# One written order for 1056 kernel steps, replaced by another: a long-convolution mixer and an MLP block on one Trainium2 core

## The chip, the cores and the metric

The kernel runs on one core of a Trainium2 chip. The core has five engines with their own instruction streams: TensorE (PE in the profile; its weight loads are listed as PEld), VectorE (DVE), ScalarE (ACT), GpSimd (POOL) and SyncE (SP). Here SP issues nearly all transfers between the chip's memory and the core's on-chip buffers; POOL issues a few. The metric is device time in microseconds (us) of one execution. Five executions of the kernel before took 307.80, 305.87, 303.96, 307.02 and 307.92 us; the median is 307.02.

## The reference

The sequence has S = 2048 positions, D = 640 channels, and the MLP has F = 1728 hidden channels. All inputs are bf16. Cut to what matters:

```
sa, ca, ga, sb, cb, gb = split(silu(c) @ w_mod, 6)       # six vectors of 640
h  = layernorm(x) * (1 + ca) + sa
# A: a long convolution
q  = h
k_shift = sum over t in 0..3 of k[s - 3 + t] * shift_k[:, 3 - t]
kv = k_shift * v
y  = irfft(rfft(kv, 4096) * rfft(ssm_k, 4096))[:2048] + kv * ssm_D
x  = x + ga * (q * y)
h  = layernorm(x) * (1 + cb) + sb
# B: two residual MLPs
u  = gelu(layernorm(h) @ w1)       # 640 -> 640
u  = four channel groups of u, shifted by +1, -1, +2, -2 positions
h  = h + u @ w2
h  = h + gelu(layernorm(h) @ w3) @ w4                    # 640 -> 1728 -> 640
x  = x + gb * B(h)
```

## The kernel before

**An order written out by hand.** The kernel's code first adds 1056 *steps* to a planner. A step is one or a few instructions on one engine, with the regions of the buffers that it reads and writes. The string ORDER (lines 26 to 67) then lists all steps as number and engine: S for SP, G for POOL, D for DVE, A for ACT, P for PE; behind a PE step stands the quarter of PSUM (0 to 3) that it allocates. The planner only replays that string. The costs in the code, such as `add("PE", 0.17 * kn, ...)`, were used when orders were searched, and issue nothing. So each engine runs its steps strictly in the order of the string: a step that waits for its data holds all later steps of that engine, and for SP that means all later transfers. Some steps name two engines in the code (for instance `("ACT", "DVE")`); the letter in the string chooses.

**Buffers.** Nearly all memory is a few large tiles that are used again and again: Ra (ssm_k first, then x), Rb, T01 (DFT data, at the end w3 and w4), R3 (a spectrum, then modulation weights, then activations), R5 (k and v, then a spectrum, then h), RG (a table for the DFT, later w1, w2 and a scratch row), RH, RK and RQ. A transfer into a tile waits until the last reader of the old content is done.

**The stages, in the order in which they start.**

1. *Tables and the spectrum of ssm_k* (0 to about 28 us). ssm_k is loaded, each of its five blocks of 128 channels is transposed by DVE (L395), and a DFT of length 4096 is done in two matmul stages: stage 1 (L408) and stage 2 (L425), each evacuated from PSUM by ACT or DVE (L208, L210). POOL builds tables and the diagonal matrices for the shift.
2. *k_shift and kv* (about 20 to 60). SP loads k and v with transposing transfers, one for each of five blocks (L234; blocks 0 to 4). PE applies the four taps with diagonal weights (L480), DVE multiplies by v (L485), DVE transposes (L395), and the two DFT stages follow (L408, L446). x is loaded by eight transfers of 320 KB (L540; four for tiles 0 to 7, four for 8 to 15), and statistics of the first layer norm are made by ACT or DVE (L554, L562) and finished on POOL (L572 to L577).
3. *Modulation*. w_mod is loaded in 12 pieces of 400 KB (L503), each multiplied by silu(c) on PE (L509) and evacuated (L516 to L526). Six go early. The last six, into R3, are i6 and i7 (for 1 + cb), i8 and i9 (sb), i10 and i11 (gb).
4. *Inverse stage 1* (69.6 to 94.5). For ten blocks, halves of the spectrum are swapped by two transfers (L629, one from SP, one from POOL), DVE makes two products (L633, 20 in all), PE multiplies by tables (L644, L645), and the result is evacuated into T01.
5. *Inverse stage 2* (L685, 97 to 123). PE turns T01 into y, in groups of two or three of the 16 row tiles: 0 to 2, 3 and 4, 14 and 15, 8 to 10, 5 to 7, 11 to 13.
6. *The chains.* The row tiles form groups of one or two. For each, chain a makes x + q*y (L761, L764) and a sum of squares on ACT (L753); ln_finish (L720 to L743) turns sums into mean and scale on POOL, or partly DVE; chain b applies cb and sb (L775, L779, L780); chain c normalizes again (L748, or L610) and turns the tile. The first groups are turned by PE (L796, with a copy, L802), the later ones by a transposing transfer from SP (L789).
7. *The MLPs.* w1 (L842, and L852 for a remainder of the channels), w2 with shifted columns (L897), its residual on DVE (L904), another layer norm and turn, w3 (L931) with gelu on ACT (L935), w4 (L961, L952), the residual (L984), gb and x (L989, L990), and four output transfers for each tile (L993). The very last tile is done in two halves (L1005 to L1011). w1 is loaded into RG at L661, w2 at L662, with four tails at L664, and w3 and w4 into T01 at L1020 to L1023.

The end of a planner's run is a plain replay:

```
order = pl.run()
with tc.manual_schedule():
    for t in order:
        t.fn(t.on)
```

Of the kernel before, what the change touches and what calls it, by code (L numbers as in the profile page):

```python
# [23 lines left out]
LFFT = 4096  # L24

ORDER = """
0S 2S 19G 18D 21G 20D 27G 29D 23D 4S 50G 28D 24A 36G 37G 22D 30A 68G 69D 25A 26G 88P:0 31A 89A 86P:1 87A 56G 90P:2 91A 72G 84P:3 5S 85A 3S 38G 39G 40A
73D 104P:0 106P:1 107A 70D 6S 49G 71D 105D 98P:2 102P:3 103A 99A 8S 118P:0 74G 94P:1 95A 75D 114P:3 115A 108P:2 109A 9S 119D 112P:0 113A 1S 66D 116P:1
41G 42G 43G 67D 80P:3 81A 117D 51D 52D 110P:2 44A 45D 10S 111D 96P:0 97A 82P:1 122P:3 11S 123D 32G 34G 54A 33S 53A 83A 76P:0 77A 100P:2 101D 92P:1 93A
78P:3 7S 120P:0 46G 136D 79A 55G 121D 175P:2 176A 47S 195P:1 196A 35S 179P:3 180A 185P:2 186D 147P:1 141P:0 193P:3 142D 148A 57G 58G 181P:2 182D 59G  # L30
139P:1 194A 140A 201S 199P:0 48S 200A 143P:3 144D 155P:2 165P:1 166D 156A 161P:0 162A 202S 191P:3 192D 12S 157P:2 158A 167P:1 168D 13S 163P:0 164A
197P:3 198A 145P:2 203S 146D 189P:1 65G 151P:0 152D 169P:3 190A 204S 183P:2 170A 184D 159P:1 160A 177P:0 178D 153P:3 154A 173P:2 174A 149P:1 150D
137P:0 260P:3 254D 171P:2 187P:1 138A 60A 188A 61G 62G 63G 261A 214D 172A 14S 124P:0 266P:1 210D 267A 125D 126P:3 127D 15S 211D 255D 209A 258P:2 259A
16S 270P:1 271A 130P:0 131D 268P:3 64A 262P:2 343G 269A 263A 215A 128P:1 264P:3 129D 256D 276P:2 277A 265A 134P:0 132P:1 17S 135D 282P:2 212A 283A
133D 216G 286P:3 223S 224P:0 220S 213G 278P:1 287D 225A 226S 279A 232S 284P:2 257D 221P:0 229S 285A 272P:3 227P:1 222A 228D 274P:2 235S 275D 273A
290P:0 291A 469D 288P:1 289A 233P:3 234D 292P:2 293A 294P:0 296P:3 230P:1 297A 298P:2 295D 299A 466D 342S 253G 246S 248G 312P:0 308P:3 309A 231D 463D
300P:1 301A 313D 460D 251G 310P:2 311D 367G 243S 306P:0 307A 316P:3 317D 280P:1 281A 252G 314P:2 304P:0 302P:3 305A 249S 240G 315D 236P:1 303A 237D
318P:2 319D 467D 340P:0 345D 241S 341A 338P:1 339A 238S 242G 326P:3 327A 344D 245S 250G 366S 322P:2 334P:0 352D 330P:1 331D 323A 244G 335A 239G 247G
324P:3 325A 346P:2 350S 351G 353D 347A 348P:0 360D 320P:3 349A 321A 328P:1 329A 354P:2 355A 359G 358S 361D 374S 356P:0 368D 369D 332P:3 333A 375G
362P:1 363A 364P:2 376D 365A 336P:3 337A 370P:1 371A 357A 372P:2 377D 378P:3 379A 380P:1 381A 383G 382S 385D 384D 386P:0 390S 391G 392D 393D 398S 373A  # L40
388P:3 387A 217A 399G 401D 394P:1 400D 425S 396P:2 397A 408D 407G 389A 402P:0 406S 409D 404P:2 395A 414S 416D 405A 415G 417D 464D 465D 426P:3 403A
427D 452S 410P:1 411A 412P:2 413A 420P:0 421D 418P:1 419A 422S 423P:3 456S 461D 470D 424D 468D 462D 218A 475P:20 477D 476A 520D 459G 454S 499D 500D
471D 521D 472A 540D 434S 219G 523D 541D 543D 437S 438P:1 439A 512A 435P:3 428S 429P:2 430A 431S 432P:0 501A 522A 433A 436A 525D 502G 504D 457S 478P:12
480A 503G 524G 526D 505D 473D 491P:03 545D 542A 544G 507D 553A 492A 527A 474D 546D 479A 571D 568D 485P:20 528G 529G 493A 530D 531P:1 506A 508G 509D
510P:3 486A 208S 547A 487A 458G 511A 548D 549G 481G 569D 570A 572D 573A 482P:20 484A 550D 551P:3 552A 532D 536P:1 533A 513D 537A 207S 574D 483D 575G
576D 580D 577D 517P:0 518A 581D 582D 583A 538P:3 578D 584G 579A 539A 585G 488P:21 489A 556P:0 557A 534D 535D 558P:3 559A 515P:2 516A 453S 514D 631D
632D 633A 586D 589D 590P:0 587P:3 455S 560P:2 634D 206S 635D 637G 591D 636A 638G 554D 561D 563D 588A 639D 562A 600P:0 601A 598P:3 599A 643D 640D 641D
642A 564G 494S 565D 644D 645D 646A 205S 441A 647D 490A 648G 566P:2 498G 567D 444D 651D 555D 605P:0 606D 607A 602P:3 649D 443D 603D 497S 652S 650S 699D
700D 447D 604A 620P:2 621A 495S 616P:1 617A 618P:0 661P:3 619A 662A 659P:2 660A 622P:1 623A 608D 609G 440D 610D 611P:0 613D 614P:3 615D 701A 663P:2
666P:1 664D 612A 683P:3 665A 667D 668A 681P:0 682A 677P:2 445G 656A 653D 654D 442G 655D 592D 669D 670G 674A 678A 671D 672P:1 673D 679P:0 680A 675P:1  # L50
593D 594D 702D 703D 496S 624P:2 595D 596D 676A 519G 597D 765D 749P:0 704A 705G 706G 766D 767A 768D 684A 707A 449A 625D 711D 747P:1 685P:32 712D 748A
769D 713D 714A 708D 709D 715D 771G 626D 446D 770A 710A 745P:1 716G 686P 717A 718S 772G 450D 719D 687D 720S 729P:3 773D 448G 750A 629S 774D 775D 777A
778D 779D 746A 727P:0 721D 781D 722D 723D 834D 835D 780A 776A 730A 627S 451G 790A 787A 657D 658D 782G 783D 743P:1 785D 791D 728A 731P:3 831D 832D 630S
688D 833A 732D 744A 733A 734P:0 735D 784S 786S 793P:1 794A 795P:3 737D 693D 694D 697S 736A 751P:02 796A 797P:1 800P:3 752P 738G 741D 836A 837G 838G
839D 753D 840D 798D 692S 739A 740S 742S 815P:0 843D 844D 801D 803D 841D 696S 813P:1 811P:3 845D 847G 842A 846A 848G 851D 788D 816A 849D 724A 725D 689S
809P:0 799A 852S 802A 804G 807D 814A 810A 812A 805D 850S 853P:1 759D 854A 808S 855P:2 856A 806S 875P:0 876A 869P:3 857P:1 873P:2 871P:0 726D 792D 874A
690S 789D 628S 754D 691S 891D 892D 894D 870A 860P:2 760D 951D 872A 895D 896A 695S 817P:30 893A 897G 898G 952D 954D 861D 862A 858D 863D 877P:21 953A
818P 903A 758S 904D 819D 899D 900D 698S 820D 859A 864G 865A 955G 905D 866S 906A 879D 822S 878P 867A 868S 933P:3 824S 901D 907G 902A 908G 909D 934A
911D 910S 956D 957D 958D 825D 912S 915P:2 935P:0 936A 913P:3 916A 763S 931P:0 757S 959A 914A 917P:2 929P:3 932A 960G 930A 961G 756S 821S 823S 962D
755S 963S 966P:0 967A 918D 919A 826D 885D 886D 920P:2 921D 830S 888S 829S 923G 762S 764S 922A 964P:1 965A 937P:30 969P:2 761S 880D 924G 968G 970D  # L60
972P:1 1003P:2 939D 925A 881S 1004D 926S 973D 975G 927A 928S 987P:3 988A 983P:2 971A 981P:1 890S 984A 1006G 974A 1005A 883S 889S 882S 827S 982A 985P:3
828S 976G 977D 1007G 938P 945D 979A 1008A 978S 980S 1010P:2 1011A 1012P:1 884S 1009S 946D 949S 1016P:0 1017A 948S 940D 942S 944S 1014P:2 943S 986A
989P:03 887S 1013A 1036P:1 991D 992D 996S 994S 1038P:0 990P 1015A 947S 997D 1034P:2 1039A 941S 1018P:03 1035A 1032P:2 1033A 998D 999S 1001S 993S 1002S
1042D 1043D 1000S 950S 1020D 1021D 1025S 1024S 1022S 1023S 1019P 1026D 1037A 995S 1027D 1031S 1029S 1030S 1028S 1040P:02 1044D 1045D 1047S 1046S 1048S
1049S 1041P 1050D 1051D 1052S 1053A 1054S 1055A
"""


# [69 lines left out]
def kernel(  # L138
# [16 lines left out]
    add = pl.add  # L155
# [5 lines left out]
    T01 = mem.tile([P, 20480], BF, name="T01")  # L161
# [272 lines left out]
    def stage2_half(h):  # L434
        for k0 in range(0, 32, 3):
            kn = min(3, 32 - k0)
            ps = Slot()

            def f(e, ps=ps, k0=k0, kn=kn):
                psv = pst(ps, name="ps_s2")[:, :, 0:480].rearrange("p g (k s) -> p g k s", k=3)  # L440
                for j in range(kn):
                    k = k0 + j
                    for cc in range(2):
                        for g in range(2):
                            p = slice(64 * g, 64 * g + 64)
                            nc.tensor.matmul(psv[:, g, j], lhsT=Gs[p, k, 64 - 64 * cc:192 - 64 * cc], rhs=T1h[h][p, cc * 32 + k],  # L446
                                             start=(cc == 0), stop=(cc == 1), tile_position=(64 * g, 0))
            t0 = add("PE", 0.17 * kn, f, r=[("T01", 10240 * h, 10240 * h + 10240), ("RG", 192 * k0, 192 * (k0 + kn))], alloc=ps, ni=8 * kn)
            w = [("R5", 10240 * h, 10240 * h + 10240, "s2"), ("kT", 4 * h, 5, "s2")] + ([("vT", 0, 5, "s2")] if h else [("kTp", 0, 1, "s2")])
            t1 = evac(XS[:, 160 * h:160 * h + 160, k0:k0 + kn, :],  # L450
                      lambda t, kn=kn: t[:, :, 0:480].rearrange("p g (k s) -> p s k g", k=3)[:, :, 0:kn], 320 * kn, ps, w)
# [268 lines left out]
    def ln_finish(li, t0, n, quick):  # L720
# [4 lines left out]
        def f(e):  # L725
            eng_of[e].tensor_scalar(nm, s1, -1.0 / D, None, ALU.mult)  # L726
            if n == 1:
                eng_of[e].tensor_scalar(rs, nm, nm, EPS, ALU.mult, ALU.subtract)
            else:
                eng_of[e].tensor_tensor(rs, nm, nm, ALU.mult)  # L730
                eng_of[e].tensor_scalar(rs, rs, -1.0, EPS, ALU.mult, ALU.add)
# [7 lines left out]
            nc.gpsimd.tensor_tensor(rs, rs, mhalf[:, 0:n], ALU.pow)  # L739
            if not quick:  # L740
                nc.gpsimd.tensor_tensor(nb, nm, rs, ALU.mult)
        add("POOL", 0.8 if quick else 1.1, f, port=-1, r=[("s2", 100 * li + t0, 100 * li + t0 + n), ("nm" + k, 0, 1)], w=[("ln" + k, 0, 1)])
        return rs, nb, ("ln" + k, 0, 1), nm, ("nm" + k, 0, 1), quick  # L743

    def normed(dst, dk, src, sk, rn, i):
# [343 lines left out]
```

## Time and profile before

| what | value |
|---|---|
| median of five executions | 307.02 us |
| profiled execution: time, span | 307.8 us, 306.0 us |
| mean granted TensorE clock | 0.966 |
| PE busy | 270.7 us, 88% |
| DVE busy | 218.1 us, 71% |
| ACT busy | 210.2 us, 69% |
| POOL busy | 111.6 us, 36% |
| moved by DMA | 35.75 MB |
| chain that ended last | PE 57%, DMA 13%, DVE 10%, ACT 6%, POOL 5%, issue 5%, SP 2% |

The span runs from the first to the last instruction of the profiled execution; its time on the device is 1.8 us longer. Times in rows count from the start of the span. A row of the trace gives start, duration, engine, line of the kernel, operation and tiles (written tile before the arrow, read tile behind it); square brackets hold the idle time of the engine before the row and what ended it. Rows "SPq" are SP's issuing of a transfer, which is not the transfer itself. In busy times by stretches, each engine's microseconds stand beside its number of instructions, then the granted clock, the busy share of the 16 DMA engines and GB/s.

### The profile page before, as it was taken

What the parts mean: (1) busy time and instruction counts of PE and PEld (TensorE: products, weight loads), DVE (VectorE), ACT (ScalarE), POOL (GpSimd) and SP (SyncE); (2) the same over time, 40 slices, a digit from 0 to 9 for tenths busy, and PEclk for the clock granted to TensorE, in tenths of its full rate; (3) what the DMA queues carried; (4) which work ended last, traced back from release to release, by engine and by line L of the source; (5) the groups of instructions that cost most, each with busy time, mean ns of one, the idle gap of its engine ahead of it and who ended that gap; (6) DMA issues with size and microseconds to landing.
All of it is one profiled execution on the core that took longest, in us unless ns stands there. A gap on an engine that the chain in (4) does not pass through costs nothing.

```text
span 306.0 us, 7648 instructions
## 1 busy us (share of the span) xinstructions
PE 270.7 (88%) x3050; PEld 207.1 (68%) x3054; DVE 218.1 (71%) x432; ACT 210.2 (69%) x352; POOL 111.6 (36%) x251
## 2 busy tenths in 40 slices
PE   0889999999889458687999989999999999999993
PEld 0555655778787136566887767688867886887771
DVE  8998999999899878879669986656474064031442
ACT  4789999999999599886768776276561752814110
POOL 4968553462104665441525660230152121400000
PEclk9999999999999855899999999999999999999999
DMA  6998999698899910642800222223014123130111
GB/s 200 261 208 181 224 184 270 185 240 217 201 266 272 249 31 3 218 129 48 287 3 1 20 47 51 54 43 77 2 20 85 26 55 70 26 86 5 32 51 43
DMA packets 58116, 35.75 MB, mean 117 GB/s; under 512 B 39873, under 2 KB 54849, under 8 KB 58081
## 3 DMA queue, kind: packets, MB, share of 16 engines
q1 hardware_dynamic: 56768, 31.55, 43.2%
q0 software_dynamic: 1216, 3.67, 4.4%
q8 instruction: 24, 0.39, 0.6%
q14 instruction: 12, 0.09, 0.1%
q10 hardware_dynamic: 96, 0.04, 0.1%
HBM read 16.31 MB, written 2.62 MB: 62 GB/s over the span
## 4 chain that ended last, share of the span: by engine, by line
PE 57%; DMA 13%; DVE 10%; ACT 6%; POOL 5%; issue 5%; SPq 2%; DVEq 0%; ACTq 0%; POOLq 0%
PE ps_w L931 18%; PE ps_w L961 15%; PE ps_w L897 5%; PE ps_ksh L480 4%; PE ps_w L842 4%; PE ps_s L408 4%; DMA R<-in_w_mod_dram 3%; ACT R L208 2%; DMA RG<-R 2%; POOL lnv L739 2%; DMA RK<-R 2%; ACT RG L753 2%; DMA RH<-RK 2%; DMA Rb<-R 2%; DVE Rb L395 1%
## 5 line engine op out<-in xcount | busy, mean ns | idle before, releaser
L931 PE MATMUL ps_w<-R,T 128*128 128x256 bf16 (+1 forms) x630 | 64.6, 261 | 1.2 <-DMA R<-RH 0.7
L931 PEld LDWEIGHTS <-T 128*128 128x128 bf16 x630 | 55.7, 98 | 8.8 <-issue 2.6
L935 ACT ACTIVATE R<-ps_w 128x1024 bf16<-128x1024 f32 (+2 forms) x36 | 29.0, 829 | 47.2 <-PE ps_w L931 47.0
L961 PE MATMUL ps_w<-T,R 128*128 128x320 bf16 x416 | 59.0, 299 | 0.0
L961 PEld LDWEIGHTS <-R 128*128 128x128 bf16 x416 | 40.3, 98 | 15.6 <-issue 0.5
L208 ACT CAST T<-ps_s 128x1024 bf16<-128x1024 f32 x34 | 32.7, 1026 | 3.3 <-PE ps_s L408 3.2
L753 ACT ACTIVATE RG<-R 128x640 bf16<-128x640 bf16 x32 | 23.6, 736 | 13.6 <-DVE R L780 9.0
L408 PE MATMUL ps_s<-F1bd,Rb 128*128 128x256 bf16 x160 | 22.3, 288 | 9.2 <-DVE Rb L395 9.0
L984 DVE TENSOR_TENSOR T<-ps_w,R 128x640 bf16<-128x640 f32 x15 | 12.3, 821 | 22.1 <-PE ps_w L952 11.5
L208 ACT CAST R<-ps_s 128x640 bf16<-128x640 f32 (+1 forms) x36 | 27.3, 844 | 0.8 <-PE ps_s L425 0.6
L408 PEld LDWEIGHTS <-Rb 128*128 128x128 bf16 x160 | 16.2, 103 | 14.9 <-DVE Rb L395 9.8
L897 PE MATMUL ps_w<-RG,R 128*128 128x320 bf16 x160 | 23.7, 302 | 0.0
L739 POOL TENSOR_TENSOR lnv<-lnv,mhalf 128x2 f32<-128x2 f32 (+1 forms) x29 | 22.6, 781 | 2.3
L842 PE MATMUL ps_w<-R,RG 128*128 128x256 bf16 (+1 forms) x200 | 21.1, 268 | 0.6 <-ACT Rb L208 0.5
L726 POOL TENSOR_SCALAR lnv<-stat 128x2 f32<-128x2 f32 (+1 forms) x14 | 4.8, 343 | 44.3 <-DVE Ra L764 17.2
L904 DVE SCALAR_TENSOR_TENSOR R<-ps_w,R 128x640 bf16<-128x640 f32 x16 | 13.0, 819 | 11.2 <-PE ps_w L897 11.2
L644 PE MATMUL ps_i<-EA,Rb 128*128 128x128 bf16 x160 | 19.2, 219 | 1.0 <-DVE Rb L633 0.8
L645 PE MATMUL ps_i<-EB,Rb 128*128 128x128 bf16 x160 | 19.0, 219 | 1.3 <-DVE Rb L633 1.3
L842 PEld LDWEIGHTS <-RG 128*128 128x128 bf16 x200 | 18.0, 107 | 2.7 <-issue 1.2
L897 PEld LDWEIGHTS <-R 128*128 128x128 bf16 x160 | 15.5, 99 | 6.2 <-issue 0.5
L208 ACT CAST T<-ps_i 128x1024 bf16<-128x1024 f32 x19 | 18.2, 1046 | 0.9 <-PE ps_i L645 0.8
L480 PE MATMUL ps_ksh<-R,RQ 128*128 128x512 bf16 x76 | 18.4, 380 | 0.4 <-POOL RQ L356 0.3
(179 smaller groups left out, 522.8 us busy)
## 6 DMA issues: line engine op xcount, KB each, us to landing
Ra<-in_A_ssm_k_dram SPq DMA_DIRECT2D x5, 512.0 KB, 5.4
Ra<-in_A_q_dram SPq DMA_DIRECT2D x8, 320.0 KB, 7.7
R<-in_w_mod_dram SPq DMA_DIRECT2D x6, 400.0 KB, 7.8
out_dram<-RH SPq DMA_DIRECT2D x60, 40.0 KB, 1.6
T<-in_B_w_dram SPq DMA_DIRECT2D x1, 2160.0 KB, 8.7
T<-in_B_w_dram SPq DMA_DIRECT2D x1, 2080.0 KB, 9.9
RH<-in_w_mod_dram SPq DMA_DIRECT2D x4, 400.0 KB, 4.2
RK<-R SPq DMA_DIRECT2D x5, 256.0 KB, 4.3
```

The costliest lines, as they stand in the source:

```text
L208: nc.scalar.copy(dst, src(ps.tile))
L408: nc.tensor.matmul(psv[:, ml, :], lhsT=xL[:, s0:s0 + P], rhs=F1r, start=True, stop=True)
L480: nc.tensor.matmul(pt[:, i, :], lhsT=diagw[:, b, jj, :], rhs=kT[:, b, c0:c0 + 512], start=(jj == 0), stop=(jj == 3))
L644: nc.tensor.matmul(psv[:, w, :], lhsT=Av[:, r_, :, g_], rhs=EAf, start=True, stop=False)
L645: nc.tensor.matmul(psv[:, w, :], lhsT=Bv[:, r_, :, g_], rhs=EBf, start=False, stop=True)
L739: nc.gpsimd.tensor_tensor(rs, rs, mhalf[:, 0:n], ALU.pow)
L753: add("ACT", 0.74, lambda e: nc.scalar.activation(junk, src, ACT.Square, scale=float(D) ** -0.5, accum_out=stat[:, li, 1, t:t + 1]), r=[sk ...
L842: nc.tensor.matmul(pt[:, fb, 0:cw], lhsT=w1_sb[:, b, 160 * fb:160 * fb + P], rhs=hT[:, b, 0:cw], start=(b == 0), stop=(b == ND - 1))
L897: nc.tensor.matmul(pt[:, hf, 0:320], lhsT=gsf[:, fb, c0:c0 + P], rhs=w2_sb[:, fb, 320 * hf:320 * hf + 320], start=(fb == 0), stop=(fb == 4))
L931: nc.tensor.matmul(pt[:, fl, 0:cw], lhsT=w3_sb[:, b, fb * P:(fb + 1) * P], rhs=xT[:, b, 0:cw], start=(b == 0), stop=(b == ND - 1))
L935: nc.scalar.activation(g3[g % 2][:, f0:f0 + fn, 0:cw], ps.tile[:, 0:fn, 0:cw], ACT.Gelu_apprx_tanh)
L961: nc.tensor.matmul(bank(i, hf), lhsT=gg[:, fb, i * P:(i + 1) * P], rhs=w4_sb[:, fb, 320 * hf:320 * hf + 320], start=(fb == 0 and i == 0), ...
```

## The change

ORDER is written out anew: the same 1056 steps, each listed once, in another sequence. Some steps with two possible engines change letter, most PSUM quarters change, and two numbers of the planner's cost table and one unused default argument change with it.

What moves, by the numbers of the steps:

- *SP, around the loads of k and v.* Steps 201 to 204 are the four x loads of tiles 0 to 7, 12 and 13 are k and v block 2, 14 to 17 blocks 3 and 4. Before: 201, 202, 12, 13, 203, 204, 14. After: 201, 204, 203, 202, 12, 13, 14.
- *SP, around the last modulation weights.* Steps 422, 425, 428, 431, 434, 437 are the loads of i6, i7, i8, i9, i10, i11; 414 is the last swap from SP; 452 is w1; 454 to 457 are the tails of w2 and 453 its main part; 205 to 208 are the x loads of tiles 8 to 15; 494 is w3. Before: 414, 452, 422, 456, 454, 434, 437, 428, 431, 457, 208. After: 414, 431, 422, 434, 456, 437, 428, 206, 207, 452, 205, 455, 457, 208, 453, 497, 454, 494. (425 comes earlier in both.)
- *PE, in the same place.* 475, 478, 491, 485, 482 and 488 are groups of inverse stage 2; 423, 426, 429, 432, 435, 438 the modulation products of i6 to i11. Before, from 475 on: 475, 438, 435, 429, 432, 478, 491, 485. After: 475, 435, 432, 438, 478, 429, 491, 485. On ACT, 501 (the first sum of squares of chain a) moves ahead of two evacuations of these products.
- *PE, later.* A w3 step of MLP group 2 (743; groups count from 0) moves ahead of the second w4 tile of group 1 (686), and a w3 step of group 1 (681) behind 749, one of group 2. Both stand before w1 group 5 (729, 727). Near the end of the w1 work, the last w1 group and w2 groups 6 to 8 move ahead of w3 steps of group 5.
- *Engines.* From ACT to DVE: some normalizations and layer-norm statistics (441, 449, 533 among them). From DVE to ACT: four copies of turned tiles (532, 567, 591, 615) and others. From POOL to DVE: seven first parts of ln_finish (528, 584, 637, 847, 897, 907, 975).
- *Start.* On ACT, two evacuations of other blocks of the first DFT come before those of block 0; on POOL one more step stands ahead of the diagonal weights; DVE has more work ahead of its first products.

The core of the diff:

```
 ORDER = """
...
-139P:1 194A 140A 201S 199P:0 48S 200A 143P:3 144D 155P:2 165P:1 166D 156A 161P:0 162A 202S 191P:3 192D 12S 157P:2 158A 167P:1 168D 13S 163P:0 164A
-197P:3 198A 145P:2 203S 146D 189P:1 65G 151P:0 152D 169P:3 190A 204S 183P:2 170A 184D 159P:1 160A 177P:0 178D 153P:3 154A 173P:2 174A 149P:1 150D
...
-427D 452S 410P:1 411A 412P:2 413A 420P:0 421D 418P:1 419A 422S 423P:3 456S 461D 470D 424D 468D 462D 218A 475P:20 477D 476A 520D 459G 454S 499D 500D
-471D 521D 472A 540D 434S 219G 523D 541D 543D 437S 438P:1 439A 512A 435P:3 428S 429P:2 430A 431S 432P:0 501A 522A 433A 436A 525D 502G 504D 457S 478P:12
-480A 503G 524G 526D 505D 473D 491P:03 545D 542A 544G 507D 553A 492A 527A 474D 546D 479A 571D 568D 485P:20 528G 529G 493A 530D 531P:1 506A 508G 509D
...
-769D 713D 714A 708D 709D 715D 771G 626D 446D 770A 710A 745P:1 716G 686P 717A 718S 772G 450D 719D 687D 720S 729P:3 773D 448G 750A 629S 774D 775D 777A
...
+136D 92P:2 34S 47S 120P:3 121D 93A 179P:1 55G 180A 46S 7S 193P:0 194A 35S 195P:2 196A 181P:1 147P:0 148A 182D 201S 141P:3 142D 139P:2 140A 143P:1
+199P:0 175P:3 200A 48S 176A 144D 204S 185P:2 186D 161P:1 162A 65G 157P:0 158D 171P:3 172A 203S 165P:2 166D 191P:1 192A 167P:0 155P:3 156A 168D 169P:2
+170A 177P:1 178D 189P:0 190A 151P:3 159P:2 160A 202S 152D 145P:1 146D 187P:0 188A 149P:3 150D 197P:2 198A 183P:1 184D 153P:0 154A 163P:3 164A 262P:2
+173P:1 174A 12S 137P:0 138A 13S 214D 263A 126P:3 56G 264P:1 210D 254D 127D 57G 124P:0 125D 211D 58G 59G 60A 61G 62G 63G 265A 260P:2 215A 266P:1 267A
+261A 14S 255D 64A 15S 128P:3 129D 258P:0 259A 270P:1 271A 130P:2 131D 256D 16S 212A 276P:0 277A 268P:1 269A 132P:3 134P:2 17S 133D 135D 257D 282P:0
...
+392D 386P:1 400D 387A 396P:2 397A 394P:0 398S 399G 401D 402P:3 425S 403A 404P:1 405A 408D 395A 426P:2 407G 406S 409D 416D 410P:3 415G 414S 417D 412P:1
+431S 411A 465D 413A 461D 462D 427D 216G 420P:0 421D 418P:3 419A 470D 422S 423P:1 424D 471D 468D 218A 475P:20 476A 477D 520D 499D 434S 456S 500D 521D
+540D 541D 543D 459G 472A 435P:3 436A 523D 473D 474D 432P:1 437S 438P:2 219G 501A 433A 512A 478P:03 439A 522A 502G 503G 428S 429P:1 430A 504D 505D 542A
+491P:21 525D 479A 524G 507D 526D 528D 492A 506A 480A 568D 527A 545D 485P:02 487A 493A 486A 206S 544G 546D 547A 207S 508G 509D 510P:3 529G 511A 530D
+531P:2 532A 482P:10 481G 569D 570A 548D 452S 571D 572D 574D 573A 458G 517P:3 518A 205S 513D 536P:2 533D 484D 549G 483A 550D 534D 575G 580D 581D 576D
+455S 582D 457S 577D 578D 208S 514D 538P:3 584D 537A 535D 634D 635D 631D 539A 583A 488P:01 551P:2 552A 579A 585G 586D 515P:3 589D 632D 449D 489A 558P:2
+516A 637D 559A 556P:0 557A 636A 453S 587P:3 633A 638G 590P:2 591A 490A 497S 588D 454S 560P:0 561D 562A 643D 600P:2 601A 639D 494S 563G 564G 598P:3
...
+594D 702D 624P:1 676A 749P:3 765D 766D 703D 704A 681P:0 747P:2 750A 682A 445G 653D 654D 655D 768D 769D 770A 705G 706G 625D 626D 767A 745P:3 685P:10
+748A 743P:2 771G 707D 708D 711D 709D 710A 686P 712D 713D 772G 773D 777A 715G 714A 716G 717A 718S 774D 778D 779D 780A 775D 776A 744A 781D 719D 720S
...
 """
...
@@ -436,7 +436,7 @@
-            def f(e, ps=ps, k0=k0, kn=kn):
+            def f(e, ps=ps, k0=k0, kn=kn, hh=h + 2):
...
-            t0 = add("PE", 0.17 * kn, f, r=[("T01", 10240 * h, 10240 * h + 10240), ("RG", 192 * k0, 192 * (k0 + kn))], alloc=ps, ni=8 * kn)
+            t0 = add("PE", 0.145 * kn, f, r=[("T01", 10240 * h, 10240 * h + 10240), ("RG", 192 * k0, 192 * (k0 + kn))], alloc=ps, ni=8 * kn)
@@ -739,7 +739,7 @@
-        add("POOL", 0.8 if quick else 1.1, f, port=-1, r=[("s2", 100 * li + t0, 100 * li + t0 + n), ("nm" + k, 0, 1)], w=[("ln" + k, 0, 1)])
+        add("POOL", 1.0 if quick else 1.3, f, port=-1, r=[("s2", 100 * li + t0, 100 * li + t0 + n), ("nm" + k, 0, 1)], w=[("ln" + k, 0, 1)])
```

## The prediction, made before the changed kernel ran

> **What bounds the kernel now.** I read the clock line first (span 306.0 us, mean granted clock 0.966; the profiled run took 307.8, so 1.8 lie around the span), then the page, where PE is busy 88% but has two weak slices near a third of the span, then busy time by stretches, then the chain of waits, then PE's and SP's rows in order of time. The stretches (start:end, length, then busy us of PE, PEld, DVE, ACT, POOL, granted clock, DMA share, GB/s):
>
> ```profile
> 100.00:104.10 4.10, 0.90 (x8) 0.42 (x6) 3.93 (x12) 1.97 (x3) 3.26 (x5) 1.00 1.12 229
> 104.10:112.00 7.90, 5.01 (x207) 2.89 (x210) 6.26 (x16) 6.29 (x15) 3.77 (x8) 0.50 0.54 130
> 112.00:121.20 9.20, 6.55 (x180) 5.26 (x165) 7.20 (x20) 8.99 (x17) 6.66 (x21) 0.50 0.01 2
> 121.20:128.00 6.80, 3.87 (x136) 3.14 (x134) 5.79 (x15) 6.62 (x16) 3.06 (x6) 1.00 0.41 119
> 128.00:131.40 3.40, 3.40 (x32) 3.17 (x30) 2.83 (x7) 2.61 (x9) 0.60 (x3) 0.50 1.02 417
> 131.40:145.00 13.60, 10.78 (x119) 8.70 (x117) 11.31 (x32) 10.20 (x24) 4.31 (x9) 1.00 0.27 57
> 145.00:177.00 32.00, 31.81 (x279) 25.48 (x279) 26.26 (x71) 23.38 (x45) 16.37 (x42) 1.00 0.28 76
> 177.00:179.00 2.00, 0.56 (x6) 0.41 (x5) 1.86 (x7) 1.47 (x4) 1.75 (x4) 1.00 0.59 123
> 179.00:256.00 77.00, 76.89 (x646) 60.30 (x645) 42.01 (x102) 44.96 (x83) 18.96 (x58) 1.00 0.20 43
> ```
>
> From 145 on PE is full, with one hole of 1.44 us at 177 and one of 0.67 at 258; from 259 to 301 it is busy 42.00 of 42.00. So a microsecond by which the middle ends earlier is a microsecond of the kernel. Between 100 and 145 PE idles, and part of its work runs at half clock. (From 28 to 60, PE, DVE and ACT are busy 31.3, 31.2 and 31.5 of 32: nothing there absorbs a delay. From 69.6 to 94.5 DVE is busy 24.0 of 24.9 with the spectral multiplies, L633.) The chain through the middle:
>
> ```profile
> 92.69 1.30 SPq L664
> ...
> 94.05 0.41 SPq L503
> ...
> 95.66 10.11 DMA R<-in_w_mod_dram
> ...
> 105.81 1.52 PE ps_mod L509 x5
> 107.33 1.10 PE ps_i L685 x54
> ```
>
> SP holds four loads of modulation weights behind a tail load of w2 (L664) that waits until 92.25 for its place; the last weights land at 105.8. PE shows who stands behind them:
>
> ```profile
> 103.54 1.00 PE L509 MATMUL ps_mod<-R,silu_w 128*128 128x320 bf16 x5 [3.20 <-DMA R<-in_w_mod_dram]
> 105.81 1.52 PE L509 MATMUL ps_mod<-R,silu_w 128*128 128x320 bf16 x5 [1.27 <-DMA R<-in_w_mod_dram]
> 107.26 2.43 PE L685 MATMUL ps_i<-T,RH 32*32 32x160 bf16 x144
> ...
> 114.46 0.71 PE L796 MATMUL ps_tr<-RG,RK 128*128 128x128 bf16 x5 [1.68 <-DVE RK L748]
> ...
> 145.19 0.70 PE L852 MATMUL ps_w1x<-R,RG 128*128 128x256 bf16 x5 [1.20 <-DMA R<-RK]
> ```
>
> The inverse stage 2 (L685) stands behind both modulation steps on PE, though it needs none of them; ACT then waits 2.60 and DVE 1.53 at 108, and all layer-norm chains start from there.
>
> **The change, part by part.** Each engine runs its steps in the written order, so only order moves; the three small edits (two planner costs, a default argument) issue nothing. By the rows, steps that change engine give DVE 221.4 us instead of 218.1, ACT 203.1 instead of 208.5, POOL 121 instead of 124 in step durations.
>
> *Start, 0 to 28.* ACT gets evacuations of two other blocks ahead of block 0 and fills its wait of 0.94 at 21.1; against it, POOL's diagonal weights (2.4 us) stand behind one more step (0.5), and DVE has 0.31 more ahead of its first products. −0.5; bounds −0.9 (the whole wait) and +0.5.
>
> *Loads of x before block 2 of k and v.* SP's row before:
>
> ```profile
> 28.53 3.02 SPq L234 DMA_TRANSPOSE R<-in_A_k_dram  x1
> ...
> 34.83 5.13 SPq L234 DMA_TRANSPOSE R<-in_A_k_dram  x1
> ```
>
> The load at 28.53 is k block 2; two more x loads of 320 KB now go ahead of it, 3.0 us at the 213 GB/s of this stretch. Its landing took 4.5 to 8.7 us by these rows. It is issued about 29.7, lands 38.3 at the longest of these times, and PE's shift of block 2 now wants it at 38.2 (before 40.6; PE runs the steps that stood before it later). Bounds 0 and +6.1 (3.0 of queue, 8.7 − 5.6 from median to worst); +0.3, by the single landing above. Queued behind it on SP are v block 2 and all of blocks 3 and 4.
>
> *Start of the multiplies at 69.6.* DVE has 0.53 more ahead of the first; its wait of 0.40 for an earlier modulation goes, and the wait of 0.90 at 77.35 for a swapped spectrum stays. 0; bounds −0.9 and +1.5 (0.53 plus the swap moved one place).
>
> *Modulation weights before w1.* This is the main part. On SP the order was: last swap, w1 (L661, 1.82 of issue at 84.8), one weight load, w2 tails from 92.25, four weight loads at 94.05. Now: weight load, weight load, last weight load ready, w2 tail, two weight loads, then x, w1 and the other tails. Three of the six go out at 84.8 to 88. The two behind the w2 tail still wait until 92.6, and land about 98.5 to 99.5 (four loads, 1.6 MB, took 10.7 us before, 150 GB/s; two are 0.8 MB, 5.3 us). PE's order has the modulations before they block the inverse stage, and ACT's first square sum stands ahead of two modulation evacuations. So the waits 3.20 + 1.27 on PE, 2.60 on ACT and 1.53 on DVE go. What is late next is DVE: it has 2.8 us more ahead of the second tile's chain. Laid out by hand with the rows' durations, the first transpose on PE is at 112.3 (before 114.5), the first w2 group at 127 (before 130.8), w1 group 4 (counted from 0), after which PE is full, at 140.8 (before 145.2). The layout gives −4.4; it has no queueing between DVE, ACT and POOL, of which DVE was 3.93 of 4.10 and ACT 8.99 of 9.20 busy in two of the stretches above. I take −3.0, two thirds; bounds −4.4 and −1.0. Cover that w1 loses: it is issued near 95.5 instead of 84.8, behind 2.24 MB, and lands 101 to 105; the first w1 product needs it at about 113. w3 is issued 122.5 to 125 and needs 8.7 us (page, 2160 KB); it is wanted at 135.
>
> *Clock.* The second row of the stretches shows the clock at 0.50 from 104.1, after PE had done 0.90 in 4.10 us, until 121.2; PE was busy 6.1 of the 6.7 us before it came back. [...]
>
> *Filler at 177.* A third-group w3 step moves before w1 group 5 and a w3 step moves behind it: that step gets 2.2 us more of PE work ahead, its chain 1.07 us more DVE work: a gap of 1.44 becomes about 0.1. −1.3; bounds −1.4 and +0.5.
>
> *Late, 250 to 260.* The gap of 0.67 behind a turned tile (DMA R<-RH) closes because w1 and w2 groups stand before that w3 step; one w4 step may wait 0.1 to 1 for an evacuation. −0.3; bounds −0.7 and +1.0. The last tile (L1005 to L1011) keeps its order; 0.
>
> Sum: −0.5 + 0.3 + 0 − 3.0 − 1.3 − 0.3 = −4.8 against the profiled 307.8, so **303.0**. The median of the five runs (307.02) is 0.8 lower and they spread over 4.0 (303.96 to 307.92). Nothing fixed in the order spreads like that; landing times do, and a run with early landings has less to gain. So I keep 303.0, which is −1.3% of the median.
>
> **Rivals.** *A wait takes the place of the one removed, no change:* ACT was busy 8.99 of 9.20 in 112 to 121 and DVE gets 3.3 us more work; or k block 2 lands 3 us later. Then −3.0 becomes 0 and the rest brings −1.8: 306.0 against the profiled run, about 306.5 with a part of the x loads' bound. For it: three engines above 97% at 28 to 60. Against: ACT sheds 5.4 us, and its 2.60 wait was in the middle.
>
> *Slower, by the clock:* the clock stays at half from the drop near 106 through the layer-norm chains until PE is full. PE has a longer hole than before between the last modulation and the first transpose (102.5 to 107.5 and 109 to 112.3 by my layout). From 114.5 to 145 its work is 2.9 + 3.9 + 1.7 + 10.8 = 19.2 us at full clock (half of the 0.50 rows counted); before it paid 2.9 + 1.7 = 4.6 for half clock, and it would pay 14.6 more. Of that the holes ending on DVE or DMA (1.68 + 0.55 + 0.42 + 1.22 + 1.20 = 5.1) absorb 5.1: +9.5, 312.5. It decides once about 6 us more work than before runs at half (4.0 of gain over 9.5/14.6), that is if the clock isn't back by about 126. For it: the clock fell a second time at 128.0, after 3.87 busy in 6.80. Against: in that stretch it had come back.
>
> **How the numbers follow.** Forecast 0.58, own range 299.8 to 305.5; rival of no change 0.17, around 306.5; rival of the clock 0.25, 309 to 314. About 1% (3.1 us, so 303.95 to 310.1) is what a measurement of this kernel can tell from no change. Of the forecast 0.44 lies below 303.95 and 0.14 above; of the second case 0.01, 0.13 and 0.03 (k late at its upper bound) lie faster, within and slower; of the third 0.04 within and 0.21 slower. Faster 0.45, same 0.31, slower 0.24. The range 299.5 to 311.0 leaves out 0.03 below and about 0.16 above.
>
> **What would show it.** PE without the waits 3.20 and 1.27 on the modulation weights and inverse stage 2 near 100; the first transpose at about 112; half clock ending near 119; w1 group 4 at 141; no gap at 177; the last PE product about 5 us earlier. Wrong: a wait of over 1 us for k block 2 near 38, multiplies that start after 70.5, or half clock beyond 126.

## The result and the profile after

The changed kernel takes 303.59 us (median of 39 executions, 301.46 to 305.99) against 307.12 for the kernel before (76 executions, 303.96 to 310.88). Compared side by side the ratio is 0.9909, with a 95% interval of 0.9890 to 0.9927: 2.8 us or 0.9% faster. The profiled execution took 302.44 us with a span of 300.7.

Busy time by stretches of the changed kernel (start:end, length, busy us of PE, PEld, DVE, ACT and POOL, granted clock, DMA share, GB/s):

```profile
97.00:100.70 3.70, 3.70 (x133) 2.42 (x107) 3.56 (x8) 3.30 (x7) 2.17 (x6) 1.00 1.08 253
100.70:104.40 3.70, 0.00 (x1) 0.00 (x1) 3.53 (x13) 3.00 (x7) 3.04 (x6) 0.80 1.11 257
104.40:113.20 8.80, 5.80 (x207) 3.02 (x207) 6.85 (x17) 6.35 (x13) 4.57 (x18) 0.50 0.31 81
113.20:116.60 3.40, 3.38 (x113) 2.79 (x114) 3.26 (x10) 3.09 (x8) 2.11 (x4) 0.50 0.02 5
116.60:120.00 3.40, 1.47 (x26) 1.34 (x24) 3.33 (x9) 3.31 (x8) 1.47 (x4) 1.00 0.00 0
120.00:126.90 6.90, 6.81 (x146) 5.93 (x144) 6.20 (x18) 6.65 (x17) 1.66 (x3) 0.51 0.43 122
177.00:179.00 2.00, 2.00 (x21) 1.73 (x18) 1.90 (x5) 1.50 (x4) 0.00 (x0) 1.00 0.51 104
179.00:256.00 77.00, 77.00 (x644) 60.17 (x643) 46.41 (x121) 41.83 (x81) 18.01 (x54) 1.00 0.23 43
```

The late part is what the prediction said: 177 to 179 is now full, and so is all of 179 to 256. The middle is not. The waits of PE for modulation weights are gone (they are done at 100.1), but PE stands still from 100.70 to 104.40, in the middle of one group of inverse stage 2. PE's rows in order of time:

```profile
97.94 2.21 PE L509 MATMUL ps_mod<-R,silu_w 128*128 128x320 bf16 x15
100.08 0.62 PE L685 MATMUL ps_i<-T,RH 32*32 32x160 bf16 x22
104.40 0.97 PE L685 MATMUL ps_i<-T,RH 32*32 32x160 bf16 x42 [3.70 <-issue]
105.30 1.51 PE L509 MATMUL ps_mod<-R,silu_w 128*128 128x320 bf16 x5
...
113.22 1.25 PE L796 MATMUL ps_tr<-RG,RK 128*128 128x128 bf16 x10 [2.40 <-POOL R L828]
...
142.31 0.71 PE L852 MATMUL ps_w1x<-R,RG 128*128 128x256 bf16 x5 [1.61 <-DMA R<-RK]
```

"issue" means that PE waited for no semaphore that the profile shows. The DMA queues of that same stretch, 100.7 to 104.4 (first the DMA engines' busy tenths in 40 slices, then packets, MB and share):

```profile
DMA  9999899999999998999999999999999999999999
...
q1 hardware_dynamic: 798, 0.93, 108.7%
q8 instruction: 1, 0.02, 2.3%
```

One packet of 16 KB came in on the instruction queue, at 101.7 to 103.1, while the DMA engines were busy with bulk loads, at 80% or more in each of the 40 slices. The whole run has 24 such packets, and PE has 6,104 matrix products and weight loads: 254 to a packet. Between the packet at 89.5 and the stall PE went through 464 recorded instructions, more than one packet's share and fewer than two. My reading, tested below, is that PE ran out of instructions, because the next packet, its next block of instructions, stood behind w1, w2 and x on the DMA engines. Inverse stage 2 would use blocks fastest: 32 small products and as many weight loads for each row tile make 1,024 instructions for the 16 tiles, some four blocks by the 254 to a packet (an estimate), within some 25 us; the packets come 3.7 to 6.4 us apart from 101.7 to 121.7, and 7.3 us or more apart elsewhere.

### The profile page after: what moved, and what is told of

Same layout as the page of the kernel before. It is cut to its first block, busy times and chain, and to the rows that moved or that the text cites. A ratio compares the mean times of both kernels' runs of the same rounds, so it can differ in the third digit from the quotient of the medians.

```text
span 300.7 us, 7654 instructions
## 1 busy us (share of the span) xinstructions
PE 270.7 (90%) x3050; PEld 206.9 (69%) x3054; DVE 220.8 (73%) x446; ACT 204.0 (68%) x345; POOL 109.3 (36%) x238
## 4 chain that ended last, share of the span: by engine, by line
PE 67%; ACT 9%; DMA 8%; DVE 7%; issue 4%; SPq 2%; POOL 2%; DVEq 0%; ACTq 0%; POOLq 0%
PE ps_w L961 17%; PE ps_w L931 16%; PE ps_w L897 6%; PE ps_w L842 5%; PE ps_ksh L480 5%; PE ps_s L408 5%; ACT T L208 4%; PE ps_s L425 3%; PE ps_mod L509 2%; ACT R L208 2%; DMA RH<-in_w_mod_dram 2%; PE ps_i L685 1%; DMA Ra<-in_A_ssm_k_dram 1%; DVE Rb L395 1%; PE ps_i L644 1%
## 5 line engine op out<-in xcount | busy, mean ns | idle before, releaser
L738 POOL TENSOR_TENSOR lnv<-stat,lnv 128x2 f32<-128x2 f32 x19 | 4.9, 255 | 63.7 <-ACT RG L753 36.3
L858 ACT ACTIVATE R<-ps_w1x 32x256 bf16<-32x256 f32 (+1 forms) x40 | 13.2, 330 | 7.9 <-PE ps_w1x L852 7.5
```

## The experiments

All ratios are to the kernel before, run beside each kernel. To set profiles side by side I use three marks on PE: the last step of inverse stage 1 (418), the start of w1 group 4 (661), and the last w4 step (1041). Edits of the order are shown as the sequence on the engine named.

### The modulation loads alone, in the old order

```
 SP
-414 452 422 456 454 434 437 428 431 457
+414 431 422 434 456 437 428 452 454 457
```

> The kernel before, with one thing of the new order: SP issues the modulation loads i9, i6 and i10 ahead of the w2 tail and i11 and i8 ahead of w1, as in the changed kernel. PE, ACT, DVE and POOL keep their old order. Theory A (the late modulation weights bound the middle, and an instruction block that PE fetches at about 101 takes part of that wait's place): PE's wait of 1.27 for weights at 105.8 goes, inverse stage 2 of tiles 3 and 4 starts near 105 instead of 107.3, PE still stands idle 3 us near 100 to 104 but the profile names no transfer for it; 1.5 to 2.5 us faster than before. Theory B (the loads were not what bound it; the gain lies in the order of the computing engines): within 0.5 us of before.

Measured: 307.19 us, ratio 1.000 (0.9964 to 1.0035). PE's rows:

```profile
99.45 2.89 PE L509 MATMUL ps_mod<-R,silu_w 128*128 128x320 bf16 x20
...
103.11 0.22 PE L685 MATMUL ps_i<-T,RH 32*32 32x160 bf16 x1 [0.48 <-ACT modv L524]
107.06 2.01 PE L685 MATMUL ps_i<-T,RH 32*32 32x160 bf16 x127 [3.73 <-issue]
```

All four products are done by 102.34; before, the last ended at 107.33. Then the stall of 3.73 takes the place of the two waits of 3.20 and 1.27 nearly whole. Theory B's number is met, but by A's mechanism: the loads did move, and the gain went into a stall for instructions.

### The modulation loads put back, in the new order

```
 SP
-414 431 422 434 456 437 428 206 207 452 205 455 457 208 453
+414 452 422 456 454 434 437 428 431 457 208 207 453 206 205 455
```

> The changed kernel, with SP's modulation loads put back behind w1 and the w2 tails in the old sequence; the other engines keep the new order. Theory A: PE waits for the weights of i10 and i9 until about 105, inverse stage 2 of tiles 3 and 4 ends near 107 instead of 105.4, and the kernel loses 1.5 to 2.5 us of its gain, about 1 us faster than before. Theory B: it stays as fast as the changed kernel, within 0.5 us.

Measured: 305.76 us, ratio 0.9954 (0.9921 to 0.9987): half of the gain is lost, as A has it.

```profile
104.77 2.85 PE L509 MATMUL ps_mod<-R,silu_w 128*128 128x320 bf16 x10 [5.09 <-DMA R<-in_w_mod_dram]
...
115.96 1.47 PE L685 MATMUL ps_i<-T,RH 32*32 32x160 bf16 x80 [4.33 <-issue]
```

PE waits 5.09 for weights and then stalls for instructions all the same, one group later. The new order of PE, with i9's product second, needs the early loads; the old one, with i9's last, needed them less. That would be why the same move of loads is worth about 1.4 us here (0.9954 against 0.9909) and nothing there.

### The filler at 177 alone, in the old order

```
 PE
-747 685 745 686 729 727 743
+747 685 745 743 686 729 727
 ACT
-748 ... 750 ... 746 730 ... 728 744
+750 748 ... 746 744 730 ... 728
```

> The kernel before, with one w3 step of MLP group 2 (743) put ahead of the second w4 tile of group 1 (686) on PE, its evacuation and that of 749 moved to suit. Theory A (the gap at 177 was PE running out of ready work for 1.4 us): the gap of 1.44 us at 177 falls to 0.2 or less and the kernel is 1.2 to 1.4 us faster than before. Theory B (PE work is only shifted, and the gap comes back at a later group): within 0.4 us of before, with a gap of over 1 us elsewhere between 179 and 256.

Measured: 306.96 us, ratio 1.0007 (0.9974 to 1.0040).

```profile
113.28 1.47 PE L685 MATMUL ps_i<-T,RH 32*32 32x160 bf16 x79 [2.96 <-issue]
...
183.32 2.62 PE L897 MATMUL ps_w<-RG,R 128*128 128x320 bf16 x18 [1.98 <-ACT R L844]
```

The gap at 177 is gone and one of 1.98 stands at 183, for a gelu that ACT has not done yet. Theory B holds here: a filler alone shifts the gap to the next group. The first row shows something else: in this profile, which has the old order unchanged up to that point, PE stalls for instructions too, at the group of tiles 8 to 10. The profile of the kernel before has no such stall.

### The last modulation product first

```
 PE
-475 435 432 438 478 429 491
+475 435 432 438 429 478 491
```

with its evacuation (430) ahead of 439 on ACT and its load (428) listed ahead of it.

> The changed kernel, with the modulation product i8 (429) ahead of inverse stage 2 of tiles 3 and 4 (478) on PE, and its evacuation (430) ahead of 439 on ACT. Theory A (PE stands 3.70 us for its next block of instructions inside 478, and i8 queued behind it holds ACT, DVE and all layer-norm chains): the stall stays, near 101 to 105, but i8 is evacuated before 103, the waits of 2.67 on ACT and 1.74 on DVE at 107 go, the first transpose on PE comes 1 to 2 us earlier than 113.2, and the kernel is 0.7 to 1.7 us faster than the changed one. Theory B (DVE and ACT are the bound there, as their 98% of busy time in parts of this stretch says): less than 0.4 us.

Measured: 303.51 us, ratio 0.9872 (0.9831 to 0.9912). That is 0.4% better than the changed kernel by the middle of the intervals, which overlap. Its profile doesn't show the mechanism as expected: 429 waits 2.23 for ACT to free its PSUM quarter, and the stalls are 1.24 and 2.71. Inconclusive.

### The bulk loads held back, in the new order

```
+    add("SP", 0.5, lambda e: nc.sync.dma_start(RG[0:1, 7872:7880], y_all[0:1, 8, 0:8]), r=[("Rb", D * 8, D * 8 + 8)], w=[("RG", 7872, 7880)])
 SP
-456 437 428 206 207 452 205 455 457 208 453
+456 437 428 452 1056 453 455 457 206 207 205 208
```

Step 1056 is the new transfer of 16 bytes into unused columns.

> The changed kernel, but SP holds the w2 loads and the four x loads of tiles 8 to 15 (2 MB in all) until the inverse stage 2 of tiles 8 to 10 is evacuated (near 111), by a transfer of 16 bytes from that result ahead of them; w1 goes directly behind the modulation loads. Theory C (PE's stall of 3.70 us at 100.7 is the fetch of its next 16 KB of instructions, which waits behind bulk transfers on the same DMA engines): the fetch near 101.7 starts 3 us or more earlier, the stall falls below 1 us, and the kernel is 1.5 to 3 us faster than the changed one (about 301 us). Theory D (the stall is PE's own and has nothing to do with traffic): the stall stays at 3 to 4 us, no gain.

Measured: **301.38 us, ratio 0.9818 (0.9762 to 0.9874)**; theory C holds and D falls. The queues at 101.0 to 104.7:

```profile
q8 instruction: 1, 0.02, 1.9%
```

It is the only queue with a packet. The block that came at 101.7 in the changed kernel comes at 99.3 here (94 to 104 has two packets on that queue, 101.0 to 104.7 one), before PE needs it. That is 2.4 us earlier, or 3.6 if it is counted from the end of inverse stage 1, which comes 1.2 us later here. No idle time put down to "issue" is shown at that place any more. PE's next wait, and what bounds this stretch now:

```profile
103.57 0.84 PE L509 MATMUL ps_mod<-R,silu_w 128*128 128x320 bf16 x5 [1.06 <-ACT modv L524]
...
112.83 1.25 PE L796 MATMUL ps_tr<-RG,RK 128*128 128x128 bf16 x10 [3.70 <-POOL R L828]
```

```profile
101.00:113.00 12.00, 5.77 (x234) 3.40 (x233) 11.44 (x31) 10.29 (x23) 8.66 (x26) 0.70 0.01 3
```

DVE is busy 11.44 of 12.00. Its wait of 1.74 for the last modulation, which the changed kernel has at 107.37, is gone. From the first mark to the second this kernel takes 46.05 us, where the three profiles of the new middle take 46.83, 47.28 and 47.66: 0.8 to 1.6 us and not the whole 3.70. DVE, busy nearly throughout, is what looks late next. The time falls by more, 2.8 us by the ratios; one profile doesn't show where the rest lies.

### The bulk loads held back, in the old order with early modulation loads

```
 SP
-456 437 428 452 454 457 208 207 453 455 206
+456 437 428 452 1056 454 457 453 455 208 207 206
```

> The kernel before with the modulation loads ahead of w1 (as in the first run of this study), and in addition w2 and three of the four x loads of tiles 8 to 15 held on SP until inverse stage 2 of tiles 8 to 10 is evacuated. Theory C: the stall of 3.73 us at 103 to 107, which took the place of the weights' wait, falls below 1 us, and now the earlier modulation loads show: 2 to 3.5 us faster than the kernel before. Theory D: the stall stays, and the time is that of the kernel before within 0.5 us.

Measured: 305.91 us, ratio 0.9989 (0.9954 to 1.0024). The stall at 103 is gone and w1 group 4 starts at 142.39, where the three profiles of the old middle have 143.63, 144.19 and 145.19. Yet the time moves by 0.1%, at most 0.5%. Behind 145 this profile has gaps of 0.80, 0.48 and 1.08. So C's mechanism shows and its size doesn't; where the rest went is open, since one profile stands against twelve executions.

### The filler taken out of the new order

```
 PE
-745 685 743 686 729 727 795 793
+745 685 686 729 727 795 743 793
```

with 744 behind 796 on ACT.

> The changed kernel, with the w3 step 743 put back behind w1 groups 5 and 6 on PE (its evacuation 744 behind 796 on ACT). Theory A (this step fills the gap ahead of w1 group 5): a gap of 1.0 to 1.5 us opens ahead of w1 group 5 near 175, 1.0 to 1.4 us slower than the changed kernel. Theory E (the gap closed because the layer-norm chain of that group runs earlier on DVE and ACT in the new order): no gap over 0.3 us, within 0.4 us of the changed kernel.

Measured: 305.75 us, ratio 0.9989 (0.9956 to 1.0021), 0.8% slower than the changed kernel.

```profile
177.88 0.71 PE L852 MATMUL ps_w1x<-R,RG 128*128 128x256 bf16 x5 [1.36 <-DMA R<-RK]
...
181.30 0.71 PE L852 MATMUL ps_w1x<-R,RG 128*128 128x256 bf16 x5 [0.54 <-DMA R<-RK]
```

Theory A holds for the gap: it opens again, at two groups. The cost is larger than A had it, some 2.5 us by the ratios where 1.0 to 1.4 was expected; from w1 group 4 to the end this one step carries 2.3 us (153.82 against 151.48).

### The clock

```
-            for fb in range(4):
+            for fb in [0, 1, 2, 3] * (2 if g == 1 else 1):
```

> The changed kernel, with the 20 matrix products of w1 group 1 (536) done twice, so that PE is busy 117.8 to 119.2 where it waits for PSUM until 119.7; the result is the same. Theory F (the clock falls to half at 120.0 because PE was busy only some 1.5 of the 3.4 us before): the clock stays at 1.0 past 120, w1 and its remainder at 120 to 127 run at full clock, 1.5 to 2.5 us faster than the changed kernel. Theory G (the half clock there runs beside ACT and DVE, which set the pace): the clock stays up but the time is within 0.5 us of the changed kernel; if the clock falls all the same, the second copy costs up to 1 us.

Measured: ratio 0.9892 (0.9849 to 0.9934), the changed kernel's within the intervals.

```profile
119.10:127.00 7.90, 5.88 (x167) 4.91 (x165) 7.62 (x21) 7.75 (x18) 1.95 (x5) 1.00 0.30 80
```

The clock stays at 1.00 after 119.1, where the changed kernel has 0.51 from 120 to 126.9. But from the last step of inverse stage 1 to w1 group 4 it takes 47.99 us, with the half clock 47.65. Theory G holds: DVE (7.62 of 7.90) and ACT (7.75) set the pace there, and PE waits for them instead of running slowly.

### Less of DVE ahead of the first tiles

```
 DVE
-473 474 504 505 ... 569 548 571
+504 505 ... 569 548 473 474 571
```

on top of the held loads.

> The changed kernel with the w2 and x loads held on SP (as in the run that held them), and in addition the two DVE steps that finish q of tile 4 (473 and 474, 0.97 us by the rows at 105.03 and 105.54 of that run) behind the layer-norm steps of tiles 0 and 1. Theory H (DVE, busy without a break from 96.6 to 113 in that run, sets the first transposes): the first transpose on PE comes 0.8 to 1.0 us earlier, and the kernel is up to 0.9 us faster than with the held loads alone. Theory I (the pace behind 113 is set by ACT, which is busy 99% there, with the same load as before): the first transpose moves and w1 group 4 doesn't; within 0.3 us.

Measured: 301.63 us, ratio 0.9847 (0.9802 to 0.9892). The first transpose is at 111.60 instead of 112.83, as H has it, and w1 group 4 at 141.15 instead of 141.90. The time is that of the held loads alone within the intervals, which are too wide to choose between H and I.

### The weights of i3

```
 PE
-294 230 310 302 312 298 308
+294 310 302 312 298 230 308
```

with its evacuation (231) moved likewise on DVE, and in another PSUM quarter.

> The changed kernel, with the modulation product i3 (230) on PE behind four steps of stage 2 of kv that don't need it. Theory J (the 1.4 us that the changed kernel is ahead at 28 us are lost at 60, where PE waits 0.95 to 2.1 us for the weights of i3): the wait near 60 goes, inverse stage 1 starts 0.8 to 1.7 us earlier, and the kernel is 0.8 to 1.7 us faster than the changed one. Theory K (the DMA engines, busy 99% from 28 to 60, or DVE in inverse stage 1 set the pace): the wait only moves, to the swaps or the multiplies, and the time stays within 0.4 us.

Measured: 304.44 us, ratio 0.9930 (0.9899 to 0.9961): no gain, as K has it. The wait moves, but to the weights of the next product, not to the swaps or the multiplies that K names:

```profile
60.63 1.84 PE L446 MATMUL ps_s<-T,RG 64*128 64x160 bf16 x48 [0.49 <-DVE T L210]
62.69 0.85 PE L509 MATMUL ps_mod<-RH,silu_w 128*128 128x320 bf16 x5 [0.22 <-ACT R L208]
64.75 0.85 PE L509 MATMUL ps_mod<-RK,silu_w 128*128 128x320 bf16 x5 [0.69 <-DMA RK<-in_w_mod_dram]
```

### Half of one order, half of the other

The first kernel lists all steps in the old order except those that the new order has behind w1 group 4 (659, its second part), which follow in the new order; the second is the reverse.

```
 all engines, first kernel
-old order
+old order, without the steps that stand behind 659 in the new order
+those steps, in the new order, with its engines and PSUM quarters
```

> The order of the kernel before up to w1 group 4 on PE (near 145), and the order of the changed kernel from there on. Theory L (most of the gain that lasts lies behind 145: from that step to the end the profiles show 153.6 to 154.8 us with the old order and 151.0 to 151.5 with the new one): 2.2 to 2.6 us faster than before. Theory A (the modulation loads in the middle are most of it, as predicted): at most 1.7 us faster, the 1.3 and 0.3 us predicted for the two late gaps.

> The order of the changed kernel up to w1 group 4 on PE, and that of the kernel before from there on. Theory L: 0.5 to 1.2 us faster than before. Theory A: 3 us faster.

Measured: 306.01 us, ratio 0.9973 (0.9935 to 1.0010), and 309.37 us, ratio 1.0073 (1.0036 to 1.0110). Both numbers of theory L fail. Of A's, the first is met (at most 1.7 us faster; 0.8 by the ratio, and the interval holds no change), and the second fails. The old middle with the new end has one wait behind 144, at the seam:

```profile
146.27 3.83 PE L842 MATMUL ps_w<-R,RG 128*128 128x256 bf16 x20 [1.93 <-ACT R L935]
```

1.93 of waiting and, at 3.83 instead of the changed kernel's 2.35 for these 20 products, 1.5 lost in the step: 3.4 us, more than the new end brings. The new middle with the old end has a seam and three gaps:

```profile
149.75 0.81 PE L796 MATMUL ps_tr<-RG,RH 128*128 128x128 bf16 x10 [1.63 <-DVE RH L748]
179.65 0.70 PE L852 MATMUL ps_w1x<-R,RG 128*128 128x256 bf16 x5 [1.29 <-DMA R<-RK]
212.55 3.44 PE L931 MATMUL ps_w<-R,T 128*128 128x256 bf16 x30 [1.38 <-DMA R<-RH]
261.76 7.80 PE L931 MATMUL ps_w<-R,T 128*128 128x256 bf16 x70 [1.03 <-DMA R<-RH]
```

An order fits the times at which its own earlier part delivers; the halves can't be priced apart by splicing.

## Why the prediction came out, point by point

The total was forecast as 303.0 and is 303.59. The parts were not what the sum said, and that the total fits is in good part luck. The marks below are over all profiles in which the stretch named (for a mark, everything up to it) is in one order or the other without an edit; up to the first mark, edits of the modulation, w1, w2 and x loads are let pass. The forecasts are summed up to each mark.

| mark or stretch | old order | new order | forecast change |
|---|---|---|---|
| last step of inverse stage 1 | 95.24 to 97.59, median 96.04 (5 profiles) | 94.66 to 98.01, median 95.93 (8) | −0.2 |
| w1 group 4 | 143.63, 144.19, 145.19 | 142.31, 144.53, 144.68 | −3.2 |
| w1 group 4 to last w4 step | 153.63, 154.07, 154.81 | 150.96 to 151.54 (7) | −1.6 |

- *Start, −0.5.* By 28 us the new order is 1.4 ahead (stage 2 starts at 26.37, before 27.76), more than forecast, and all but 0.1 of it is gone at 96 by the medians. PE's waits near 60 for the i3 weights are 0.95 us in the changed kernel and 2.43 in the second of the halved kernels. The run with i3 later shows that they only move on. The step that failed is leaving out who is late next at 60.
- *x loads, +0.3, and the start of the multiplies, 0.* Right in this profile: no wait for block 2, whose steps started at 38.46 and 40.64 without one, and the multiplies start at 69.37 (before 69.63). In other profiles they start as late as 72.60 with the new order and 71.55 with the old, so the sign "after 70.5" tells nothing.
- *Modulation weights, −3.0.* The loads do move PE's waits of 3.20 and 1.27 away, as described, but ACT's 2.60 and DVE's 1.53 come back as 2.67 and 1.74 at 107, for the last product, which is queued behind the stall. The size is wrong: about 0 at w1 group 4 by the medians (144.5 against 144.2), not −3.0. The failed step is the layout by hand, which let PE run through inverse stage 2 and gave no time to the fetch of its instructions: 3.70 us. In the profile of before this fetch fell into the wait for weights (its packet came at 101.0 to 102.3, the wait ran to 103.5) and cost nothing there. But that profile is not typical. From the first mark to the second it takes 49.79, while the two other profiles of the old middle take 46.60 and 47.59: they wait at most 1.12 at a time for weights, and stall 2.96 and 2.68 for instructions at tiles 8 to 10. The new middle takes 46.83, 47.28 and 47.66. So the −3.0 was also priced on one long middle. With the bulk loads held, w1 group 4 starts at 141.90 and 141.15 in the new order, 2.3 and 3.0 earlier than the old median; but it starts at 142.39 with the loads held and only the modulation loads moved. No run holds the bulk loads and leaves the modulation loads late, so how much of this is theirs is not shown.
- *What is late next: DVE.* Right only once the stall is gone: with the bulk loads held it is 95% busy at 101 to 113. In the changed kernel PE's instructions came first.
- *Clock.* I took the row (back 6.7 us after the first transposes, so at 119); PE was busy 5.73 of those 6.7 us, not 6.1. In the changed kernel's profile the clock came back at 116.6, 3.4 us after the first transposes at 113.2, in which PE was busy 3.38 of 3.40, so the 6.7 us did not carry over. Then it fell again, from 120.0 to 126.9, so the sign "half clock beyond 126" came up. It cost nothing that shows: with full clock from 119.1 on, w1 group 4 came no earlier. In the run with i8 first the clock stayed at half from 106.5 to 127.0 (20 products of w1 took 2.34 us at 119.5 and 1.28 at 129.1), much as the rival of the clock has it, and from the first mark to the second it took 47.12, within the range of the others. With that this rival falls, and with it its assumption that half clock on PE lies on the path there.
- *Filler, −1.3, and late, −0.3.* Right in mechanism for the filler, too small: 2.8 us together by the medians (154.07 against 151.27). No run tests the late one alone. The old end loses 2.1 to 3.2 us in gaps, at different groups in different profiles (177 and 258 in one; 177, 185, 210 and 259 in another), and the new end 0 to 0.5. I priced the two gaps of one profile; the term is the looseness of that whole stretch.
- *Rival of no change.* It had a new wait take the place of the old one, on ACT or for k block 2. A wait did take the place, on PE's instruction stream, and the case came true for the middle only.

So the sum of −4.8 was too large, by 1.3 against the medians (−3.5) and by 2.0 against the ratio (−2.8): about 3 us too much in the middle, about 1 us too little at the end. It stood against a profiled execution 0.7 above the median, and that, not the sum, brought the total back to within 0.6 of the measured one.

## What to carry to other kernels

A wait that ends on a transfer can hide a second one beneath it, as the waits of 3.20 and 1.27 us for weights hid one for instructions that took 3.73 once they were gone: before pricing its removal, look at what else falls due in that time on the same engine, its instruction fetch included. Here a stretch of many small TensorE instructions ran beside bulk loads that could come later, and PE stalled for 3.70 us; holding 2 MB of loads by one tiny dependent transfer gave 0.6 to 0.9% more in the new order (ratios 0.9847 and 0.9818 against 0.9909), about as much again as the whole change. It took the stall away in the old order too, but there no gain was left at the end (0.9989). Price a loose stretch by the gaps of several profiles rather than the one at hand, and don't expect a single step of a better order, or half of it, to bring its share.

## What the runs showed of the hardware

The instruction fetch of TensorE was not expected. With the bulk loads in place PE stalled inside the group of tiles 3 and 4 for 3.70 us in the changed kernel, 3.73 with the early loads in the old order, 3.77 in the second of the halved kernels and 4.91 with i3 later. In four other kernels the stall was 2.68 to 4.33 at the group of tiles 8 to 10 (with i8 first, with the loads put back, with the filler in the old order, and in the first of the halved kernels). The kernel before, with these loads in place, shows none in its profile. In order of time, the first of these stalls begins after 2,237 of PE's recorded instructions in the changed kernel (2,241 with the early loads in the old order), the second after 2,493 with the loads put back: 256 apart, near the 254 to a packet. In the changed kernel the stall ends 1.35 us after the packet has landed on the instruction queue (104.40 and 103.05). In the three kernels that hold the loads, no stall for "issue" is left at either group.

The mean granted clock goes with the time within one kernel: over the 12 executions without the filler, 0.01 more of clock goes with 2.2 us less (correlation −0.84; over the twelve kernels of the experiments it lies between −0.07 and −0.91). The run that kept the clock up by extra work shows that, at least at 120 to 127, the clock is not what sets the time. That it falls because PE waits longer is my reading and was not tested.
